# A spectral layer with maxout on one core: where a transform's columns land in PSUM, and when the next batch's first stage runs

## The chip, the cores and the metric

One Trainium2 chip, one of its cores. The time is device microseconds of one execution of the whole kernel; a kernel is judged by the median of its runs. Engines are named as in the profile: PE is TensorE (PEld its weight loads), DVE is VectorE, ACT is ScalarE, POOL is GpSimd, SP is SyncE, which here only issues DMAs.

## What is computed

A Fourier layer over 3072 time steps of 8 batches, 256 features wide, and a maxout layer behind it:

```python
X = np.fft.rfft(x, axis=1)                      # x: 8 x 3072 x 256
Yr = Xr @ w_r - Xi @ w_i + b_r                  # 256 x 256 weights
Yi = Xr @ w_i + Xi @ w_r + b_i
Yr, Yi = (np.sign(Y) * np.maximum(np.abs(Y) - 0.01, 0) for Y in (Yr, Yi))
y = np.fft.irfft(Yr + 1j * Yi, n=3072, axis=1)
h = np.maximum(np.maximum(y @ w1, y @ w2), y @ w3)   # 256 -> 768, three times
out = h @ w_out                                 # 768 -> 256
```

## The kernel before

Each batch's 3072 steps are split as 96 x 32 (n1 and n2), and every f32 matrix product is made of three f16 products (high part times high part, high times low, low times high: `mm3`, lines 176 to 178). A batch passes through these steps:

- **Stage a**, eight times a batch (one *quad* is four values of n2): `load_x` brings the rows of x by four DMAs of SP, `sum_x` adds or subtracts two halves on DVE (`xq`, line 529), `split_x` makes the high part on ACT and the low part on DVE (`xhl`), `stage_a` transforms over n1 by 12 matmuls into two PSUM tiles `pa` (line 572), copied out by two ACT instructions (`aq`, line 579) and written to DRAM by four DMAs of POOL.
- **Stage b**, twelve blocks a batch: `load_a` reads the rows back, `split_a` splits and moves them (`ab`), `stage_b` transforms over n2 by 16 matmuls into a PSUM tile `px` (line 731), each 128 rows by 64 columns. The last of the twelve blocks is *plain*: it is laid out in another way, as is all of batch 0.
- **Stage w** multiplies by the weights (tiles `py`), adds the bias and applies the threshold (`u`); `finish_w` splits the result (`vb`), and its rows are moved by four DMAs of SP (line 850) to where **stage q** needs them. Stage q takes two blocks at once, by 12 matmuls into two PSUM tiles `pz` (line 886), which ACT copies out (`zs`), to DRAM.
- **The inverse over n1** (`load_z`, `split_z`, `inverse`: tiles `zh`, `zl`, then `pi`, evacuated as `yh` by ACT and `yl` by DVE) and **the maxout layer** (`up`: tiles `pu`; `down`: tiles `pd`) for eight chunks of six *slots* each.

The last step sets the order of everything else: the main loop runs over 8 batches x 48 slots. In a slot stand three groups of 6 matmuls of `up` (which ACT `c`, line 980, then DVE `c`, line 983, and DVE `h`, line 986, read out of PSUM) and 9 matmuls of `down`. The steps of the following batches are put between these groups: each is an event with a position in slots (`at(p, fn, ...)`), the list of events is sorted, and `run_until` issues what is due. For a batch whose stages b to q run from slot 48(b-1), stage b of block k+1 stands at 2.8(k+2) + 1 behind that slot, stage q of a pair at 2.8(k+2) + 3.2 for even k: both every 5.6 slots. The quads of batches 3 to 7 come every 5.6 slots too, one batch of slots ahead of that batch's stage b. An instruction put off with `later` is issued some thirds of a slot later; the final order on each engine is that of the scheduler, and each engine runs its instructions in that order.

PSUM: `up` has three tiles, `down` two, and all others (`pa`, `px`, `py`, `pz`, `pi` and `pt`, by `ff_tile`) share three in turn, so a tile can be written once the third tile before it has been read out. SBUF: `xq` has two buffers; the second half of x, `ab` and `vb` share eight (`raw_tile`).

Of the kernel before, what the change touches and what calls it, by code (L numbers as in the profile page):

```python
# [98 lines left out]
def fourier_maxout_kernel(  # L99
    ctx: ExitStack, tc: tile.TileContext, x, w_r, w_i, b_r, b_i, w1, w2, w3, w_out, fa, ga, mb, mq, ident, out  # L100
):
    nc = tc.nc
# [4 lines left out]
    KD = D // P  # L107
# [5 lines left out]
    SLOTS = NCH * NF  # L113
# [28 lines left out]
    def later(fn):  # L142
        if "slot" in st:
            waiting.append((st["slot"], fn))
        else:
            fn()
# [17 lines left out]
    def split_later(hi, lo, src, scale=None):  # L164
        h = hi if hi.dtype == F16 else hi.bitcast(F32)
        if scale is None:
            nc.scalar.activation(out=hi, in_=src, func=AF.Copy)
            later(lambda: nc.vector.tensor_tensor(out=lo, in0=src, in1=h, op=ALU.subtract))
        else:
            nc.scalar.activation(out=hi, in_=src, func=AF.Copy, scale=scale)  # L170
            later(lambda: low(nc.vector.scalar_tensor_tensor(  # L171
                out=lo, in0=src, scalar=scale, in1=h, op0=ALU.mult, op1=ALU.subtract
            )))
# [9 lines left out]
    def ff_tile(name):  # L183
        tag = spare[0]
        if len(spare) > 1:
            spare.append(spare.pop(0))
        return ps.tile([P, 512], F32, name=name, tag=tag, bufs=2 if tag == "dn" else 3)
# [24 lines left out]
    def raw_tile(name):  # L212
        return ffn.tile([P, 1536], F32, name=name, tag="raw", bufs=8)
# [4 lines left out]
    def s_tile(name):  # L218
        return fft.tile([P, D], F32, name=name, tag="s", bufs=3)
# [230 lines left out]
    def at(pos, fn, i, k=None, n=None):  # L450
        if n is None or 0 <= k < n:
            events.append((pos, len(events), fn, i))

    def batch(b, kind):
        if (b, kind) not in st:
            if kind in "az":
                st[b, kind] = dram.tile([96, N2, D], F32, name=kind + "_d")
            else:
                w = 2 * NCH if kind == "x" else NJP if b else 2 * NJP
                st[b, kind] = fft.tile([P, w], F32, name="mx" + kind, bufs=3)  # L460
        return st[b, kind]
# [186 lines left out]
    def plain(k):  # L648
        return k < NJP or k % NJP == NJP - 1


    def first_b(k):
        aj = st.pop(("a", k))
        px = ff_tile("px")
        pv = px.rearrange("p (h j m) -> p h j m", h=KD, j=2)
        for j in range(2):
            for h in range(KD):
                nc.tensor.matmul(
                    pv[:, h, j], aj[:, j, h * P:(h + 1) * P], mb_f[:, 2 * k + j], start=True, stop=True
                )  # L660
        st["t", k] = t = fft.tile([P, KD, 384], F32, name="tf", tag="t2", bufs=2)
        tv = t.rearrange("p h (j m) -> p (h j) m", j=2)
        nc.scalar.activation(
            out=tv[:, :, 64:192], in_=px.rearrange("p (g m) -> p g m", m=P), func=AF.Copy
        )
        nc.scalar.activation(
            out=tv[:, :, 0:64], in_=px.rearrange("p (g m) -> p g m", m=P)[:, :, 64:128], func=AF.Copy,
            scale=-1.0,
        )
        if k == NJP - 1:  # L670
            st["ts"] = s_tile("tsf").rearrange("p (h m) -> p h m", h=KD)
            st["late"] = nc.gpsimd.tensor_copy(out=st["ts"], in_=t[:, :, 192:320])
            for z in (32, 96):
                nc.gpsimd.memset(st["ts"][:, :, z:z + 1], 0.0)
# [43 lines left out]
    def stage_b(k):  # L718
        if k < NJP:
            return first_b(k)  # L720
        ah = st.pop(("as", k))
        kb = k % NJP
        px = ff_tile("px")
        if plain(k):
            pv = px.rearrange("p (h j c q m) -> p h c j q m", h=KD, j=2, c=2, q=2)
        else:
            pv = px.rearrange("p (h c q m j) -> p h c j q m", h=KD, c=2, j=2, q=2)
        for g in range(4):
            for h in range(KD):
                for i in range(2):  # L730
                    nc.tensor.matmul(  # L731
                        pv[:, h, :, g // 2, g % 2], ah[:, g // 2, g % 2, h * P:(h + 1) * P],
                        mb_sb[:, i, 4 * kb + g].rearrange("p (c m) -> p c m", c=2),
                        start=i == 0, stop=i == 1,
                    )
        t2 = fft.tile([P, 2, KD, 384], F16, name="tt", tag="t2", bufs=2)
        st["t", k] = tt = [t2[:, i] for i in range(2)]
        if not plain(k):
            split_later(
                *(t[:, :, 0:256] for t in tt), px.rearrange("p (h m) -> p h m", h=KD), T_SCALE  # L740
            )
            pc = px.rearrange("p (h c m) -> p h c m", h=KD, c=2)
            s = s_tile("s").rearrange("p (h m) -> p h m", h=KD)
            nc.scalar.activation(out=s, in_=pc[:, :, 0, :], func=AF.Copy, scale=T_SCALE)

            def third():
                nc.vector.scalar_tensor_tensor(
                    out=s, in0=pc[:, :, 1, :], scalar=T_SCALE, in1=s, op0=ALU.mult, op1=ALU.add
                )
                split_later(*(t[:, :, 256:384] for t in tt), s)  # L750

            later(third)
            return
        tv = [t.rearrange("p h (j m) -> p (h j) m", j=2) for t in tt]
        split_later(*(t[:, :, 64:192] for t in tv), px.rearrange("p (g m) -> p g m", m=P), T_SCALE)

        def rest():
            for t in tv:
                nc.gpsimd.tensor_scalar(
                    out=t[:, :, 0:64], in0=t[:, :, 128:192], scalar1=-1.0, scalar2=1.0,  # L760
                    op0=ALU.mult, op1=ALU.mult,
                )
            sp = []
            for t in tt:
                s = fft.tile([P, D], F16, name="ts", bufs=2).rearrange("p (h m) -> p h m", h=KD)
                nc.gpsimd.tensor_copy(out=s, in_=t[:, :, 192:320])
                for z in (32, 96):
                    nc.gpsimd.memset(s[:, :, z:z + 1], 0.0)
                sp.append(s)
            st["ts"] = sp  # L770

        later(rest)
# [63 lines left out]
    def finish_w(k):  # L836
        b, kb = divmod(k, NJP)
        u = st.pop(("u", k))
        st["v", k] = u
        if b:  # L840
            if plain(k) or kb % 2 == 0:
                st["vb"] = raw_tile("vb").bitcast(F16)
            v = st["vb"][:, 2048:3072].rearrange("p (i j d) -> p i j d", i=2, j=2)
            moved = st["vb"][:, 0:2048].rearrange("p (g i j d) -> p g i j d", g=2, i=2, j=2)
            split_later(v[:, 0], v[:, 1], u, st[b, "sv"][0])

            def move():
                for j in range(2):
                    for c in range(2):
                        nc.sync.dma_start(out=moved[c::2, kb % 2, :, j], in_=v[j::2, :, c])  # L850

            if not plain(k):
                later(move)
            st["v", k] = [v[:, i] for i in range(2)] if plain(k) else moved
            nc.vector.tensor_reduce(
                out=batch(b, "u")[:, kb:kb + 1], in_=u.rearrange("p j d -> p (j d)"), axis=AX.X,
                op=ALU.max, apply_absolute_value=True,
            )
# [41 lines left out]

    for q in range(EARLY, NB * NCH):
        b, i = divmod(q, NCH)
        p = i if b == 1 else 9 + 5.2 * i if b == 2 else (b - 2) * SLOTS + 5.6 * i + 2
        at(p - (3 if b == 1 else 5 if b == 2 else 8), load_x, q)
        if q >= HALF_X:
            at(p - 1, sum_x, q)
        at(p, split_x, q)
        at(p + 1, stage_a, q)
        if q >= HALF_X:
            p = 9 + 5 * i if b == 3 else (b - 3) * SLOTS + 5.5 * i + 5  # L910
            at(p - 4, load_m, q)
            at(p, largest_m, q)
            if i == NCH - 1:
                at(p + 1, scale_m, b)
    for b in range(1, NB):
        for k in range(-2, NJP + 1):
            p = 8 + 2.2 * (k + 2) if b == 1 else (b - 1) * SLOTS + 2.8 * (k + 2)
# [291 lines left out]
```

## Time and profile before

| | us |
|---|---|
| median of 3 runs | 2040.73 (2039.59, 2040.73, 2047.87) |
| the profiled execution's own time | 2044.31 |
| its span in the profile | 2042.3 |

The profile is of one execution. Its first 139 us load, split and transform batch 0; then come eight stretches of about 247 us, one for each batch of the maxout layer, the last two of them shorter since no batches are left to prepare. Where one engine is busy nearly all the time, the time goes down only where that engine does less or waits less.

### The profile page before, as it was taken

To read this page: it belongs to the slowest core of one execution; us is meant where nothing else is said; L and a number is where in the kernel's file an instruction comes from. 1 tells how busy PE (TensorE), PEld (TensorE's weight loads), DVE (VectorE), ACT (ScalarE), POOL (GpSimd) and SP (SyncE) were. 2 spreads that over 40 slices of the span, in tenths; PEclk is the share of its full clock that TensorE was granted. 3 is DMA by queue.
4 is the path that set the end of the run, shared out by engine and by line. 5 is a ranking of instruction groups with operands and counts; after the bars stand their busy time and mean duration, and the time that the engine had idled before them with its cause. 6 is when DMAs were issued, how large, how long until landed. Compare 5 with 4: busy or idle time off the path is not lost.

```text
span 2042.3 us, 42196 instructions
## 1 busy us (share of the span) xinstructions
PE 2015.8 (99%) x16335; PEld 1406.8 (69%) x16335; DVE 1487.7 (73%) x2809; ACT 1036.1 (51%) x2060; POOL 282.5 (14%) x510
## 2 busy tenths in 40 slices
PE   9989999999999999999999999999999999999999
PEld 5757777676766766666766767667667677776666
DVE  3887887788877878678876788767777577754544
ACT  4755554555545554455554565545554454543333
POOL 0000101111111121111121121211121100100000
PEclk9999999999999999999999999999999999999999
DMA  8745444465443554545544454443542333211110
GB/s 278 212 147 155 142 128 118 126 158 132 130 143 95 144 159 107 145 119 139 142 133 113 124 162 120 140 117 89 152 123 70 88 92 88 81 58 32 32 32 24
DMA packets 183798, 244.66 MB, mean 120 GB/s; under 512 B 26350, under 2 KB 142702, under 8 KB 183502
## 3 DMA queue, kind: packets, MB, share of 16 engines
q1 hardware_dynamic: 150798, 166.44, 31.2%
q0 software_dynamic: 25168, 68.59, 10.1%
q10 hardware_dynamic: 7632, 6.95, 1.1%
q8 instruction: 128, 2.10, 0.4%
q14 instruction: 72, 0.59, 0.1%
HBM read 124.16 MB, written 75.50 MB: 98 GB/s over the span
## 4 chain that ended last, share of the span: by engine, by line
PE 87%; DVE 3%; DMA 3%; issue 3%; ACT 2%; SPq 1%; POOL 0%; ACTq 0%; DVEq 0%; POOLq 0%
PE pu L176 17%; PE pu L178 17%; PE pu L177 17%; PE pd L178 6%; PE pd L177 6%; PE pd L176 6%; PE px L731 3%; PE py L178 2%; PE py L176 2%; PE py L177 2%; PE pz L886 1%; PE pa L589 1%; PE pi L178 1%; PE pi L176 1%; PE pi L177 1%
## 5 line engine op out<-in xcount | busy, mean ns | idle before, releaser
L176 PE MATMUL pu<-yh,wuh 128*128 128x384 f16 x2304 | 754.7, 328 | 1.4 <-ACT c L980 0.7
L178 PE MATMUL pu<-yh,wul 128*128 128x384 f16 x2304 | 751.5, 326 | 0.0
L177 PE MATMUL pu<-yl,wuh 128*128 128x384 f16 x2304 | 751.4, 326 | 0.0
L170 ACT ACTIVATE hh<-h 128x384 f16<-128x384 f32 x384 | 200.7, 523 | 579.1 <-DVE h L986 566.6
L983 DVE TENSOR_TENSOR c<-pu,c 128x384 f32<-128x384 f32 x384 | 212.6, 554 | 187.6 <-PE pu L178 156.3
L178 PEld LDWEIGHTS <-wul 128*128 128x128 f16 x2304 | 225.4, 98 | 149.8 <-issue 0.9
L176 PEld LDWEIGHTS <-wuh 128*128 128x128 f16 x2304 | 227.6, 99 | 141.8 <-issue 30.4
L176 PE MATMUL pd<-woh,hh 128*128 128x256 f16 x1152 | 313.8, 273 | 0.0
L177 PE MATMUL pd<-wol,hh 128*128 128x256 f16 x1152 | 313.8, 273 | 0.0
L178 PE MATMUL pd<-woh,hh 128*128 128x256 f16 x1152 | 313.4, 273 | 0.0
L171 DVE SCALAR_TENSOR_TENSOR hh<-h,hh 128x384 f16<-128x384 f32 x384 | 213.8, 557 | 131.8 <-ACT hh L170 129.2
L177 PEld LDWEIGHTS <-wuh 128*128 128x128 f16 x2304 | 227.8, 99 | 115.1 <-issue 3.6
L980 ACT ACTIVATE c<-pu 128x384 f32<-128x384 f32 x384 | 187.7, 489 | 140.1 <-PE pu L178 134.0
L986 DVE TENSOR_TENSOR h<-pu,c 128x384 f32<-128x384 f32 x384 | 211.8, 552 | 54.5 <-PE pu L178 51.6
L1017 POOL DMA_DIRECT2D out_dram<-o x189 | 104.6, 558 | 1054.3 <-ACT o L1015 1048.7
L176 PE MATMUL py<-wch,tt 128*128 128x256 f16 x504 | 137.4, 273 | 0.0
L178 PE MATMUL py<-wch,tt 128*128 128x256 f16 x504 | 137.4, 273 | 0.0
L177 PE MATMUL py<-wcl,tt 128*128 128x256 f16 x504 | 137.3, 272 | 0.0
L582 POOL DMA_DIRECT2D a_d<-aq x160 | 93.7, 590 | 309.7 <-ACT aq L579 307.0
L176 PEld LDWEIGHTS <-hh 128*128 128x128 f16 x1152 | 112.7, 98 | 33.8 <-issue 0.3
L177 PEld LDWEIGHTS <-hh 128*128 128x128 f16 x1152 | 112.7, 98 | 33.4
L178 PEld LDWEIGHTS <-hh 128*128 128x128 f16 x1152 | 112.7, 98 | 13.7 <-DVE hh L171 0.5
(226 smaller groups left out, 2854.1 us busy)
## 6 DMA issues: line engine op xcount, KB each, us to landing
zq<-z_d SPq DMA_DIRECT2D x63, 384.0 KB, 4.0
out_dram<-o POOLq DMA_DIRECT2D x189, 128.0 KB, 2.1
ab<-a_d SPq DMA_DIRECT2D x84, 256.0 KB, 4.3
ab<-ab SPq DMA_DIRECT2D x336, 64.0 KB, 2.2
vb<-vb SPq DMA_DIRECT2D x308, 64.0 KB, 2.5
z_d<-zs POOLq DMA_DIRECT2D x70, 256.0 KB, 3.9
xm<-in_x_dram SPq DMA_DIRECT2D x40, 384.0 KB, 3.7
a_d<-aq POOLq DMA_DIRECT2D x160, 96.0 KB, 2.9
```

The source lines that it names most:

```text
L170: nc.scalar.activation(out=hi, in_=src, func=AF.Copy, scale=scale)
L171: later(lambda: low(nc.vector.scalar_tensor_tensor(out=lo, in0=src, scalar=scale, in1=h, op0=ALU.mult, op1=ALU.subtract)))
L176: nc.tensor.matmul(o, lh, rh, start=start, stop=False, **kw)
L177: nc.tensor.matmul(o, lh, rl, start=False, stop=False, **kw)
L178: st["mm"] = nc.tensor.matmul(o, ll, rh, start=False, stop=stop, **kw)
L582: nc.gpsimd.dma_start(out=av[1 - r, :, :, n:n + 512], in_=o[64 * h:64 * h + 48])
L589: nc.tensor.matmul(pa[0:96], fr, xp, start=True, stop=True)
L731: nc.tensor.matmul(pv[:, h, :, g // 2, g % 2], ah[:, g // 2, g % 2, h * P:(h + 1) * P], mb_sb[:, i, 4 * kb + g].rearrange("p (c m) -> p c ...
L980: st["act"] = nc.scalar.activation(out=c1, in_=p, func=AF.Copy)
L983: st["dve"] = nc.vector.tensor_tensor(out=c1, in0=p, in1=c1, op=ALU.max)
L986: st["dve"] = nc.vector.tensor_tensor(out=h32, in0=p, in1=st["c1"], op=ALU.max)
L1017: q.dma_start(out=out_v[b, c, t], in_=o)
```

## The change

Three lines. The first changes the order of the columns of `px` in the eleven blocks of a batch that are not plain: before, the two values of j (index `g // 2`) are the innermost index, so that one matmul's 64 columns go to every second f32 of the PSUM tile; now j stands outside q and m, and the 32 columns of each half go side by side. The rows of `py`, `u` and `v` follow that order. The second line is the matching source of the moves of `v`: 64 adjacent partitions instead of every second one, 128 x 2 x 256 values in four DMAs as before, into every second partition as before. The third takes 2 off the position p of the quads of batches 3 to 7: `load_x` at p - 8, `sum_x` at p - 1, `split_x` at p and `stage_a` at p + 1 all come two slots sooner; `load_m` and `largest_m`, which have a p of their own, stay.

```diff
@@ stage_b
         if plain(k):
             pv = px.rearrange("p (h j c q m) -> p h c j q m", h=KD, j=2, c=2, q=2)
         else:
-            pv = px.rearrange("p (h c q m j) -> p h c j q m", h=KD, c=2, j=2, q=2)
+            pv = px.rearrange("p (h c j q m) -> p h c j q m", h=KD, c=2, j=2, q=2)
@@ finish_w
             def move():
                 for j in range(2):
                     for c in range(2):
-                        nc.sync.dma_start(out=moved[c::2, kb % 2, :, j], in_=v[j::2, :, c])
+                        nc.sync.dma_start(out=moved[c::2, kb % 2, :, j], in_=v[64 * j:64 * j + 64, :, c])
@@ the events of the quads
     for q in range(EARLY, NB * NCH):
         b, i = divmod(q, NCH)
-        p = i if b == 1 else 9 + 5.2 * i if b == 2 else (b - 2) * SLOTS + 5.6 * i + 2
+        p = i if b == 1 else 9 + 5.2 * i if b == 2 else (b - 2) * SLOTS + 5.6 * i
         at(p - (3 if b == 1 else 5 if b == 2 else 8), load_x, q)
```

What that does to the order, at three places of the fifth batch of slots (the same places come in the batches of slots 1 to 5, counted from 0).

**PE, slot 20 of the batch.** Before, a quad's stage a (`pa`, line 572, with the two tiles 16509 and 16510) stands right before a pair's stage q (`pz`, line 886, tiles 16530 and 16531):

```order
L572 LDWEIGHTS zeros_72
L572 MATMUL pa_16510<-xhl_16427,zeros_72 64x512
L886 LDWEIGHTS zeros_72
L886 MATMUL pz_16530<-vb_16181,zeros_72 64x512
L886 LDWEIGHTS zeros_72
L886 MATMUL pz_16530<-vb_16181,zeros_72 64x512
L886 LDWEIGHTS zeros_72
L886 MATMUL pz_16530<-vb_16181,zeros_72 64x512
L886 LDWEIGHTS zeros_72
L886 MATMUL pz_16531<-vb_16181,zeros_72 64x512
```

Now the same pair (tiles 16536 and 16537) follows the maxout layer's `pd`:

```order
L178 LDWEIGHTS hh_16341
L178 MATMUL pd_16520<-woh_83,hh_16341 128x256
L886 LDWEIGHTS zeros_72
L886 MATMUL pz_16536<-vb_16187,zeros_72 64x512
L886 LDWEIGHTS zeros_72
L886 MATMUL pz_16536<-vb_16187,zeros_72 64x512
L886 LDWEIGHTS zeros_72
L886 MATMUL pz_16537<-vb_16187,zeros_72 64x512
```

The quad's stage a has gone two slots ahead. The tiles that share the three PSUM buffers follow each other there before as py_16458, pa_16509, pa_16510, pz_16530, pz_16531, so pz_16531 takes the buffer of pa_16509; now as px_16373, py_16453, py_16479, pz_16536, pz_16537.

**PE, slot 35 of the batch.** Before, block 11 of stage b (`px`) follows a group of `up`:

```order
L178 LDWEIGHTS wul_82
L178 MATMUL pu_17688<-yh_17107,wul_82 128x384
L731 LDWEIGHTS ab_17206
L731 MATMUL px_17698<-mb_all_77,ab_17206 128x2x32
L731 LDWEIGHTS ab_17206
L731 MATMUL px_17698<-mb_all_77,ab_17206 128x2x32
```

Now a quad's stage a stands between the two:

```order
L572 LDWEIGHTS zeros_72
L572 MATMUL pa_17704<-xhl_17643,zeros_72 64x512
L731 LDWEIGHTS ab_17211
L731 MATMUL px_17724<-mb_all_77,ab_17211 128x2x32
L731 LDWEIGHTS ab_17211
L731 MATMUL px_17724<-mb_all_77,ab_17211 128x2x32
```

The tiles in the three shared buffers are there before pi_17593, py_17613, pi_17661, px_17698, and now pi_17668, pa_17703, pa_17704, px_17724: this `px` now takes the buffer of the second `pi` of slot 34, which ACT and DVE read out as `yh` and `yl`.

**DVE, slot 34 of the batch.** Before, from the slot's `c` to the read-out (`yl`) of that second `pi`:

```order
L983 TENSOR_TENSOR c1_17583<-pu_17632,c1_17583 128x384
L776 TENSOR_SCALAR t_17629<-u_17626 128x512
L986 TENSOR_TENSOR h32_17648<-pu_17641,c1_17583 128x384
L777 TENSOR_TENSOR u_17626<-u_17626,t_17629 128x512
L171 SCALAR_TENSOR_TENSOR hh_17650<-h32_17648,hh_17650 128x384
L855 TENSOR_REDUCE mxu_15743<-u_17626 128x1
L171 SCALAR_TENSOR_TENSOR vb_17537<-u_17626,s0v_11363,vb_17537 128x512
L171 SCALAR_TENSOR_TENSOR yl_17592<-pi_17661,yh_17591 128x384
```

And now:

```order
L983 TENSOR_TENSOR c1_17591<-pu_17634,c1_17591 128x384
L833 TENSOR_TENSOR u_17628<-u_17628,bias_ri_86 128x512
L171 SCALAR_TENSOR_TENSOR xhl_17643<-xq_16979,xx_14891,xhl_17643 112x512
L776 TENSOR_SCALAR t_17631<-u_17628 128x512
L171 SCALAR_TENSOR_TENSOR xhl_17643<-xq_16979,xx_14891,xhl_17643 112x512
L777 TENSOR_TENSOR u_17628<-u_17628,t_17631 128x512
L986 TENSOR_TENSOR h32_17655<-pu_17648,c1_17591 128x384
L171 SCALAR_TENSOR_TENSOR yl_17600<-pi_17668,yh_17599 128x384
```

The two `xhl` of the quad have moved in ahead of `yl`, while `hh`, `mxu` and `vb` have moved behind it; in slot 33, ahead of what is shown, the quad's two `xq` (line 529) have moved in as well.

## Rows read from the trace of the kernel before

**Rows 1.** The page's first part, busy time and share of the span of PE, its weight loads, DVE, ACT and POOL.

```profile
PE 2015.8 (99%) x16335; PEld 1406.8 (69%) x16335; DVE 1487.7 (73%) x2809; ACT 1036.1 (51%) x2060; POOL 282.5 (14%) x510
```

**Rows 2.** Busy time by stretch: the stretch, its length, then busy us (and instructions) of PE, PEld, DVE, ACT, POOL, the granted share of TensorE's full clock, the busy share of the DMA engines, GB/s. One batch of slots in the middle.

```profile
1126.00:1373.00 247.00, 244.99 (x2083) 171.57 (x2082) 192.31 (x356) 128.79 (x259) 41.90 (x74) 1.00 0.47 131
```

**Rows 3.** Waits of PE alone, longest in total first: the waiting tile and line, the releaser, us in total, times, longest.

```profile
PE pz L886 <- ACT aq L579: 10.1, 15, 1.1
PE pi L176 <- ACT zh L170: 2.4, 1, 2.4
...
PE px L731 <- DVE yl L171: 1.0, 1, 1.0
```

**Rows 4.** Timeline of PE at a block of stage b that is not plain, and the first matmul behind it: start us, us, instruction (x16: sixteen of them merged).

```profile
543.19 1.06 PE L731 MATMUL px<-mb_all,ab 128*128 128x64 f16 x16
544.06 0.35 PE L176 MATMUL pu<-yh,wuh 128*128 128x384 f16 x1
```

**Rows 5.** The same at a plain block, and the start of another batch's plain block, three batches later.

```profile
556.84 0.63 PE L731 MATMUL px<-mb_all,ab 128*128 128x64 f16 x16
557.31 0.33 PE L176 MATMUL pu<-yh,wuh 128*128 128x384 f16 x1
...
1297.94 0.63 PE L731 MATMUL px<-mb_all,ab 128*128 128x64 f16 x16
```

**Rows 6.** Line 731 alone, weight loads and matmuls of all 84 blocks: count, shortest, median and longest duration in ns, first and last start.

```profile
L731 PEld LDWEIGHTS <-ab x1344: 95/125/125, 172.3 to 1783.2; 128*128 128x128 f16 x192
L731 PE MATMUL px<-mb_all,ab x1344: 192/247/247, 172.5 to 1783.2; 128*128 128x64 f16 x192
```

**Rows 7.** Timeline of PE at a stage a and at a stage q that each stand alone.

```profile
1060.42 0.33 PE L177 MATMUL pu<-yl,wuh 128*128 128x384 f16 x1
1060.58 0.33 PE L178 MATMUL pu<-yh,wul 128*128 128x384 f16 x1
1060.84 0.84 PE L572 MATMUL pa<-xhl,zeros 48*64 48x512 f16 x12
1061.61 0.34 PE L176 MATMUL pu<-yh,wuh 128*128 128x384 f16 x1
...
1063.67 0.84 PE L886 MATMUL pz<-vb,zeros 64*64 64x512 f16 x12
1064.45 0.34 PE L176 MATMUL pu<-yh,wuh 128*128 128x384 f16 x1
```

**Rows 8.** Timeline of PE at the four places of one batch of slots where a stage q stands one group of `up` behind a stage a (the first and the last) or directly behind it (the two between); in brackets the idle time before and its releaser.

```profile
938.71 1.15 PE L886 MATMUL pz<-vb,zeros 64*64 64x512 f16 x12
939.79 0.34 PE L176 MATMUL pu<-yh,wuh 128*128 128x384 f16 x1
...
968.13 0.84 PE L572 MATMUL pa<-xhl,zeros 48*64 48x512 f16 x12
968.80 0.59 PE L886 MATMUL pz<-vb,zeros 64*64 64x512 f16 x3
970.01 0.84 PE L886 MATMUL pz<-vb,zeros 64*64 64x512 f16 x9 [0.61 <-ACT aq L579]
970.78 0.34 PE L176 MATMUL pu<-yh,wuh 128*128 128x384 f16 x1
...
999.11 0.84 PE L572 MATMUL pa<-xhl,zeros 48*64 48x512 f16 x12
...
1002.21 0.34 PE L176 MATMUL pu<-yh,wuh 128*128 128x384 f16 x1
...
1032.40 0.40 PE L886 MATMUL pz<-vb,zeros 64*64 64x512 f16 x2
...
1033.90 0.34 PE L176 MATMUL pu<-yh,wuh 128*128 128x384 f16 x1
```

**Rows 9.** Timeline of ACT at the second of these places.

```profile
968.75 0.72 ACT L170 ACTIVATE vb<-u,s0v 128x512 f16<-128x512 f32 x1
969.38 1.06 ACT L579 ACTIVATE aq<-pa 128x512 f32<-128x512 f32 x2
```

**Rows 10.** Timeline of DVE in slots 33 to 36 of the fifth batch of slots (the first row is slot 33's `h`, the fifth the `yl` of slot 34's second `pi`), and of PE at the group of `up` that writes again the buffer of slot 33's `h`.

```profile
1290.59 0.54 DVE L986 TENSOR_TENSOR h<-pu,c 128x384 f32<-128x384 f32 x1
...
1296.34 0.56 DVE L171 SCALAR_TENSOR_TENSOR hh<-h,hh 128x384 f16<-128x384 f32 x1
1296.81 0.68 DVE L855 TENSOR_REDUCE mxu<-u 128x1 f32<-128x512 f32 x1
1297.41 0.74 DVE L171 SCALAR_TENSOR_TENSOR vb<-u,s0v,vb 128x512 f16<-128x512 f32 x1
1298.07 0.55 DVE L171 SCALAR_TENSOR_TENSOR yl<-pi,yh 128x384 f16<-128x384 f32 x1
...
1299.00 1.54 DVE L529 SCALAR_TENSOR_TENSOR xq<-x,sign,xq 112x512 f32<-112x512 f32 x2
...
1303.19 1.42 DVE L171 SCALAR_TENSOR_TENSOR xhl<-xq,xx,xhl 112x512 f16<-112x512 f32 x2
...
1293.52 0.33 PE L176 MATMUL pu<-yh,wuh 128*128 128x384 f16 x1
```

**Rows 11.** The moves of `v` (line 850) by all their DMAs, from issue to landing, and the last of them ahead of the stage q at 968.80.

```profile
DMA to landing us min/median/max: 1.9/2.5/5.3
...
956.46 3.38 SPq L850 DMA_DIRECT2D vb<-vb  x4
```

## The prediction

> **What bounds the kernel now.** I read the page's busy shares first. PE is busy for 2015.8 of 2042.3 us, DVE for 73% and ACT for 51% [rows 1]. A share over the whole span hides stages, so I read the busy times by stretch next: in a batch of slots in the middle of the run PE is busy for 244.99 of 247.00 us, at the full granted clock (1.00, so 2.4 GHz) [rows 2]. So nearly all the time is PE's own, and there are two ways to shorten it: fewer nanoseconds for the same matmuls, or fewer waits between them. The list of PE's waits shows how little waiting the profile counts: the largest entry is stage q's `pz`, which waits for the read-out `aq` of stage a, 15 times and 10.1 us in all; everything else is 2.4 us or less [rows 3]. These 15 are three in each of five batches, the five in which the quads of batches 3 to 7 run. Last I read the timeline of PE at the places that the change touches, by starts alone: the ends of matmuls are modelled, so what a block costs is the time from its first start to the first start behind it.
>
> **Part one, the columns of `px`.** The trace has both layouts. A block that is not plain starts at 543.19 and the next matmul at 544.06: 0.87 us for 16 matmuls, 54 ns each [rows 4]. The plain blocks, which already write their columns side by side, take from 556.84 to 557.31: 0.47 us, 29 ns each [rows 5]. Both have the same 16 loads of 128x128 weights and the same 16 matmuls of 64 columns. The difference is 0.40 us a block. The change gives the plain blocks' spacing of columns to the 11 other blocks of batches 1 to 7, 77 in all: 77 x 0.40 = 30.8 us off PE. All of it counts, since the blocks lie in stretches in which PE has no idle time to give [rows 2]. Bounds: nothing, if something other than the columns makes the 54 ns; 30.8 if it is they. I take 30.8, since the plain blocks are the same instructions in the same kernel.
>
> What could make the 54 ns instead is the weight load. Its records have a median of 125 ns and a shortest of 95 [rows 6], yet loads and matmuls overlap, and the plain block gets sixteen of both into 0.47 us [rows 5]; a load stretched to 125 ns is then a load that waits for the matmul before it.
>
> The Trainium skill ("TensorE: Matmul & The Clock Gate", section on LDWEIGHTS) has a rule that speaks against this part: a load takes its number of columns divided by 1.2 GHz, by an estimate from it 107 ns for these 128, whatever the matmul writes, so 16 of them would take 1.7 us and the first term would be zero. Both kinds of block in this trace are shorter than that, so the trace doesn't agree.
>
> The readers of `px` on ACT and DVE read whole runs of 128 or 256 columns before and after, and cost the same. The rows of `u` and `v` come in another order, and only the source of the moves changes, from every second partition to 64 adjacent ones. No row shows exactly this pair; the moves before land 2.5 us after issue, at worst 5.3 [rows 11]. What would a slower move cost? The last of the moves ahead of the stage q at 968.80 has been issued by 959.84 (956.46 + 3.38) and lands at about 962.3, 6.5 us early. Even the worst landing, doubled, ends 1.6 us after that point, and at the median doubled nothing waits. I take zero.
>
> **Part two, the quads two slots sooner.** Each quad's events move together: four loads on SP, two sums on DVE, two splits each on ACT and DVE, 12 matmuls, two read-outs on ACT and four writes on POOL. PE's own work stays: a stage a that stands alone takes 0.77 us (1060.84 to 1061.61), a stage q alone 0.78, and PE spends 0.10 us more at the entry of such a block (0.26 from the last start before it, where 0.16 is usual) [rows 7].
>
> What goes is the meeting of the two. Both take two of the three shared PSUM tiles, so when stage q comes right behind stage a its second tile is the buffer of stage a's first, which ACT must read out; at the second place ACT is still at `vb` when stage a ends and reads out its two tiles from 969.38 to 970.44 [rows 9], and stage q goes on at 970.01, after the first [rows 8]. The profile counts 0.61 us as idle there; the starts say more. At the four places of a batch [rows 8]:
> - 938.71 to 939.79: 1.08 us instead of 0.78, 0.30 lost;
> - 968.13 to 970.78: 2.65 for both blocks. Apart they would take 0.77 + 0.78 and one more entry of 0.10, 1.65: 1.00 lost;
> - 999.11 to 1002.21: 3.10 instead of 1.65: 1.45 lost;
> - 1032.40 to 1033.90: 1.50 instead of 0.78: 0.72 lost.
>
> That is 3.47 us a batch and 17.4 us in five, against the 10.1 us that the list of waits has for them [rows 3]: the modelled ends hide the rest. In the new order no pair's stage q has a stage a among the three tiles ahead of it, so I take all 17.4. Bounds: 0 (another wait at the same places) and 17.4.
>
> **What comes in its place.** Stage a now stands right ahead of a block of stage b six times a batch. `px` takes one tile, not two, so it needs the third tile back from it, that is the tile before stage a's two. At five of the six places that was read out long ago. At slot 35 it is the second `pi` of slot 34, and there DVE is late: from the `h` at 1290.59 to the end of `yl` at 1298.62 it goes nearly from one instruction into the next [rows 10]. In the new order the quad's two `xq` (1.54 us) and two `xhl` (1.42) come ahead of that `yl`, and `hh`, `mxu` and `vb` (0.56, 0.68, 0.74) go behind it: 2.96 - 1.98 = 0.98 us later, 1299.60. `px` would start at 1297.94 [rows 5] plus stage a with its entry, 0.87 [rows 7], which is 1298.81, and so waits for about 0.8 us. In five batches 4.0 us. That such a wait exists is seen once: `px` waits 1.0 us for `yl` [rows 3]. Bounds: 0, if DVE catches up by then, and 1.5 us a batch, if the read-out on ACT is late too: 0 to 7.5.
>
> The other moves lie under cover. The loads of x move two slots ahead with their readers, so their lead stays; a slot is (1297.94 - 556.84) / 3 / 48 = 5.15 us [rows 5]. The first quad of batch 3 is now loaded before the last of batch 2 and takes the `xq` buffer in its place; that last load waits for a split of the same slot and still has five slots, 25 us. SP's and POOL's instructions are no more than before. On ACT two `aq` now come ahead of the read-out of `px`, 1.06 us [rows 9]; stage w reads that block 3.8 slots behind its stage b (2.8 + 2 - 1), some 19 us, and ACT has 118 us to spare in a stretch [rows 2], so nobody waits for it.
>
> **Sum.** -30.8 - 17.4 + 4.0 = -44.2 us. The profiled execution took 2044.31 us in its own time, so it would take 2000.1. It lies 3.6 us above the median of the runs, 2040.73, on which I put the forecast: 2040.73 - 44.2 = 1996.5, say 1997 us.
>
> **The rivals.**
> - *The waits of part two only change their place.* DVE is busy for 192 of 247 us [rows 2], and in slots 33 and 34 the quad adds its 2.96 us where DVE had no pause; were PE to lose some 3.5 us a batch there and in like places, part two would give nothing: 2040.73 - 30.8 = 2010. For it: the one place worked out above. Against: the read-outs of `up` have room (the `h` that ends at 1291.13 is needed at 1293.52, 2.4 us later [rows 10]), which is more than one move of 1.54 us takes.
> - *The 54 ns are not the columns.* If weight loads pace the blocks, or anything else that both layouts share, part one gives nothing: 2040.73 - 17.4 + 4.0 = 2027. Against: the 0.87 us beside the 0.47 [rows 4, 5]. This is where the rule of the Trainium skill above would lead.
> - *Slower.* The place is DVE's `c` and `h`, whose late end holds back the next group of `up`. All 40 moved quads would have to cost more than 48.2 / 40 = 1.2 us each to lose both gains. With a room of 2.4 us that takes a lag of 3.6 us at each quad, and a quad has 2.96 us of work on DVE: it decides only if all of that and another instruction come ahead of the same `h`. A time of 2051 or more would need 1.5 us a quad.
> - *Nothing changes.* Something that I don't see paces the slots, and the time stays near 2040. Against: PE's idle time in a stretch is 2 us of 247 [rows 2].
>
> **How the numbers follow.** My forecast, both gains less a small new wait: 0.78 (its own range 1990 to 2003: the new wait at its bounds gives 1992.5 and 2000, and the runs spread by 1 us below the median and 7 above). Waits moved: 0.14. Columns not the cause: 0.03. Nothing: 0.03. Slower: 0.02. The range of 1988 to 2011 takes in the first two cases and leaves out 0.08 and their tails. About 0.5%, 10 us, is what a measurement here can tell from no change: faster by more than that means under 2030.5, which the first three cases give, 0.95; same 0.03; slower 0.02.
>
> **What would show it.** Part one: every block of line 731 takes 0.47 us from its first start to the next matmul, and PE's matmuls there have one duration, near 192 ns. Part two: `pz` no longer stands in the list of PE's waits, and each stage q takes 0.78 us. The new wait: `px` waits for `yl`, five times, some 0.8 us each. I am wrong if the blocks stay at 0.87 us, if entries of `pu` waiting for DVE's `c` or `h` come up in PE's list, or if more places than the one at slot 35 hold `px` back.

## The result, and the profile after

The changed kernel takes 1993.38 us, the median of four runs (1992.19 to 1994.02), beside 2040.16 for the kernel before on the same chip: a ratio of 0.9762, with a 95% interval of 0.9738 to 0.9786. That is 46.8 us less; the forecast's sum was 44.2 less, which it put at 1997 us. The profiled execution took 1993.83 us in its own time, with a span of 1992.1.

The page's first part, which answers to [rows 1]:

```profile
PE 1973.4 (99%) x16335; PEld 1368.6 (69%) x16335; DVE 1482.1 (74%) x2809; ACT 1026.7 (52%) x2060; POOL 279.1 (14%) x510
```

The counts of instructions are those of before. PE's busy time is 42.4 us less and the share stays 99%: the kernel is as bound by PE as it was. One batch of slots, by stretch with the columns of [rows 2]:

```profile
1088.46:1327.54 239.08, 239.00 (x2082) 166.05 (x2080) 191.41 (x355) 127.22 (x259) 41.06 (x74) 1.00 0.51 135
```

A batch takes 239.08 us where it took 247.03 on the mean of three (741.10 / 3 from [rows 5]), 7.95 less. The granted clock is 1.00 in both, the 2.4 GHz level, so the clock has no part in it.

**The blocks of `px`.** Line 731 with all its loads and matmuls (count, shortest, median and longest ns), which answers to [rows 6], and PE's timeline at a block right behind a stage a:

```profile
L731 PEld LDWEIGHTS <-ab x1344: 95/98/100, 170.6 to 1732.8; 128*128 128x128 f16 x192
L731 PE MATMUL px<-mb_all,ab x1344: 189/193/203, 170.7 to 1732.8; 128*128 128x64 f16 x192
```

```profile
962.84 0.84 PE L572 MATMUL pa<-xhl,zeros 48*64 48x512 f16 x12
963.61 0.64 PE L731 MATMUL px<-mb_all,ab 128*128 128x64 f16 x16
964.09 0.33 PE L176 MATMUL pu<-yh,wuh 128*128 128x384 f16 x1
964.25 0.33 PE L177 MATMUL pu<-yl,wuh 128*128 128x384 f16 x1
```

The median matmul is recorded with 193 ns instead of 247, and a block takes 0.47 to 0.48 us (963.61 to 964.09) instead of the 0.87 of [rows 4]. The weight loads went from 125 ns to 98 with no change of their own, so the longer figure held time spent waiting behind the matmuls.

One part of a block's cost does not lie in the block. Before, the row behind those of [rows 4] was

```profile
544.25 0.33 PE L177 MATMUL pu<-yl,wuh 128*128 128x384 f16 x1
```

so the first matmul of `up` behind a slow block took 0.19 us from its start to the next (544.06 to 544.25), where it takes 0.16 now (964.09 to 964.25). By the starts of all records it is 190 ns behind each of the 77 slow blocks, and 163 behind the plain ones and behind every block now. Inside a slow block the matmuls follow each other by 55.8 ns, only the second comes 29 ns after the first; inside a fast one by 29.2. So each of the sixteen cost 26.7 ns more, the last of them at the expense of the matmul behind: 0.427 us a block, not 0.40.

**The meetings of stage a and stage q.** PE's waits, the first four, which answer to [rows 3], and two of the four places of [rows 8]:

```profile
PE pi L176 <- ACT zh L170: 2.4, 1, 2.4
PE pz L712 <- DVE col L262: 1.8, 1, 1.8
PE px L658 <- DMA aj<-a_d: 1.5, 2, 1.2
PE px L731 <- DVE yl L171: 1.4, 1, 1.4
```

```profile
973.96 0.84 PE L886 MATMUL pz<-vb,zeros 64*64 64x512 f16 x12
974.74 0.34 PE L176 MATMUL pu<-yh,wuh 128*128 128x384 f16 x1
...
1004.33 0.84 PE L886 MATMUL pz<-vb,zeros 64*64 64x512 f16 x12
1005.10 0.34 PE L176 MATMUL pu<-yh,wuh 128*128 128x384 f16 x1
```

The entry of `pz` behind `aq`, 10.1 us, is gone, and each stage q that takes two blocks lasts 0.77 or 0.78 us. The four entries that are left lie at the start of the run or at single places.

**What came in its place.** The list shows no new wait in the five batches, but the starts do. PE at slots 29 and 35 of the fifth batch of slots, and DVE ahead of each:

```profile
1231.07 1.09 PE L572 MATMUL pa<-xhl,zeros 48*64 48x512 f16 x12
1232.09 0.64 PE L731 MATMUL px<-mb_all,ab 128*128 128x64 f16 x16
...
1260.45 0.84 PE L572 MATMUL pa<-xhl,zeros 48*64 48x512 f16 x12
1261.37 0.63 PE L731 MATMUL px<-mb_all,ab 128*128 128x64 f16 x16
```

```profile
1230.74 0.74 DVE L171 SCALAR_TENSOR_TENSOR xhl<-xq,xx,xhl 112x512 f16<-112x512 f32 x1
...
1254.32 0.54 DVE L986 TENSOR_TENSOR h<-pu,c 128x384 f32<-128x384 f32 x1
...
1260.78 0.54 DVE L171 SCALAR_TENSOR_TENSOR yl<-pi,yh 128x384 f16<-128x384 f32 x1
```

At slot 29 stage a takes 1.02 us instead of 0.77: it starts at 1231.07, and the second half of its own low part, `xhl`, is being written until 1231.48. At slot 35 `px` starts 0.92 us behind stage a instead of 0.77, 0.05 us after the end of `yl` (1261.32). Together 0.40 us; in three of the five batches just these two come, with 0.04 more in the third quad's stage a. The first batch has 0.68, the last none. In all 1.98 us: 0.65 at the `px` of slot 35, 1.33 in stages a.

### The profile page after: what moved, and what is told of

Same layout as the page of the kernel before. It is cut to its first block, busy times and chain, and to the rows that moved or that the text cites. A ratio compares the mean times of both kernels' runs of the same rounds, so it can differ in the third digit from the quotient of the medians.

```text
span 1992.1 us, 42215 instructions
## 1 busy us (share of the span) xinstructions
PE 1973.4 (99%) x16335; PEld 1368.6 (69%) x16335; DVE 1482.1 (74%) x2809; ACT 1026.7 (52%) x2060; POOL 279.1 (14%) x510
## 4 chain that ended last, share of the span: by engine, by line
PE 90%; DVE 5%; DMA 3%; ACT 1%; issue 1%; SPq 0%; DVEq 0%; ACTq 0%
PE pu L176 18%; PE pu L178 18%; PE pu L177 18%; PE pd L178 6%; PE pd L176 6%; PE pd L177 6%; PE py L176 3%; PE py L177 3%; PE py L178 3%; PE px L731 2%; PE pa L572 1%; PE pz L886 1%; PE pa L589 1%; PE pi L178 1%; PE pi L176 1%; PE pi L177 1%
```

## The experiments

All were held against runs of the kernel before on their own chip: 2041.89 us for the columns alone, the quads alone, the even pairs and the columns four apart; 2041.76 for the moves alone, the meetings, the changed kernel again and all splits sooner; 2042.16 for the odd pairs and the two quads sooner.

**Each part alone.** First the columns with the matching moves, without the quads:

```diff
-            pv = px.rearrange("p (h c q m j) -> p h c j q m", h=KD, c=2, j=2, q=2)
+            pv = px.rearrange("p (h c j q m) -> p h c j q m", h=KD, c=2, j=2, q=2)
...
-  nc.sync.dma_start(out=moved[c::2, kb % 2, :, j], in_=v[j::2, :, c])
+  nc.sync.dma_start(out=moved[c::2, kb % 2, :, j], in_=v[64 * j:64 * j + 64, :, c])
```

> The kernel before with the new columns of px and the new source of the moves; the quads stay where they were. Theory (each part gives its own gain): 77 blocks lose 0.40 us each, 30.8 us, so about 2009.5 us against 2040.2; line 731 takes 0.47 us a block, and pz waits for aq 15 times as before. Rival (the columns don't set the 0.87 us, the whole gain of 46.8 us came with the quads): near 2040. Second rival (the parts help each other, so that shorter blocks alone only lengthen the waits of pz): 2015 to 2025.

Measured 2011.27 us, 30.6 less (ratio 0.9851, 0.9836 to 0.9867). Summed over all 1344 matmuls from each start to the next on PE, line 731 went from 69.98 us to 39.17: 30.8 less, which is the term of the prediction. The matmuls of `up` behind the 77 blocks gave 2.1 us more (190 to 163 ns each). The waits of `pz` were still there and a little longer, 0.95 us by the starts:

```profile
PE pz L886 <- ACT aq L579: 10.8, 15, 1.4
```

Then the quads alone:

```diff
-        p = i if b == 1 else 9 + 5.2 * i if b == 2 else (b - 2) * SLOTS + 5.6 * i + 2
+        p = i if b == 1 else 9 + 5.2 * i if b == 2 else (b - 2) * SLOTS + 5.6 * i
```

> The kernel before with the quads of batches 3 to 7 two slots sooner and nothing else. Theory: the blocks of line 731 stay at 0.87 us; pz leaves the list of PE's waits; by the starts of the changed kernel pa and pz together lost 16.5 us, so about 2024 us against 2040.2, and not 2030, which the 10.1 us of the list would give. Rival (the waits only change their place while px is slow, as the blocks of px then end later against DVE and ACT): 2035 to 2040.

Measured 2024.69 us, 17.2 less (0.9914, 0.9898 to 0.9929); `pz` has left the list and line 731 keeps its 247 ns. The two gains alone make 47.8 us, and both together made 46.8 and, in a second set of runs below, 48.0: the parts neither help nor hinder each other. The rival by which the waits only change their place would have shown here at 2035 to 2040.

**What about the columns costs.** Three layouts of the `px` of the kernel before, each with its moves unchanged; where the columns are paired, the moving operand is viewed in pairs too, its values in the same order. First pairs of columns:

```diff
-            pv = px.rearrange("p (h c q m j) -> p h c j q m", h=KD, c=2, j=2, q=2)
+            pv = px.rearrange("p (h c q a j e) -> p h c j q a e", h=KD, c=2, j=2, q=2, e=2)
...
```

> The kernel before, with the columns of px written in pairs: two neighbouring columns, then a gap of two. The moves are unchanged, so v's rows are permuted and the output is another; the work is the same. First theory (what costs is to go to a new pair of columns, 8 bytes, for each single column): pairs are as fast as runs, blocks of 0.47 us and about 2009.5 us. Second theory (any gap costs): blocks stay at 0.87 us and the time near 2040. The Trainium skill speaks for the first in one place ("Advanced Engine Details and Errata", section PSUM Cachelines: every two consecutive elements should be contiguous for best throughput) and for the second in another ("PSUM — Partial Sum Buffer", table at the top: any non-contiguous access pattern slows matmuls).

Measured 2011.50 us (0.9849, 0.9831 to 0.9866), the same as with columns all side by side. Then single columns four apart:

```diff
-            pv = px.rearrange("p (h c q m j) -> p h c j q m", h=KD, c=2, j=2, q=2)
+            pv = px.rearrange("p (h c m q j) -> p h c j q m", h=KD, c=2, j=2, q=2)
```

> The kernel before, with the columns of px written four apart instead of two apart; moves unchanged, so v's rows are permuted and the output is another; the work is the same. If each single column costs the same whatever the gap: blocks of 0.87 us and the time near 2040. If the cost grows with the gap: blocks above 0.87 us, at twice the extra (1.27 us) some 31 us above 2040, 2071.

Measured 2041.25 us (0.9997, 0.9988 to 1.0007): no dearer than two apart. Last pairs that begin at an odd column:

```diff
-            pv = px.rearrange("p (h c q m j) -> p h c j q m", h=KD, c=2, j=2, q=2)
+            pv = px.rearrange("p (h c q a s) -> p h c q a s", h=KD, c=2, q=2, s=4)
...
+                    j, q = divmod(g, 2)
...
-                        pv[:, h, :, g // 2, g % 2], ah[:, g // 2, g % 2, h * P:(h + 1) * P],
+                        pv[:, h, :, j, q] if plain(k) else pv[:, h, :, q, :, 0:4:3] if j else pv[:, h, :, q, :, 1:3],
+                        ah[:, g // 2, g % 2, h * P:(h + 1) * P],
...
```

> The kernel before with the columns of px in pairs that begin at an odd column: the first eight matmuls of a block write columns 1 and 2 of every four, the last eight columns 0 and 3, which in order of writing are 0, then 3 and 4, 7 and 8 and so on. Moves unchanged, so v's rows are permuted and the output is another; the work is the same. If a neighbour is all that a column needs: blocks of 0.47 us as with even pairs, 30.8 us below the kernel before, some 2010 us. If the two must share an aligned 8 bytes, as the Trainium skill's word "cachelines" would have it ("Advanced Engine Details and Errata", section PSUM Cachelines): blocks of 0.87 us and no change, some 2041 us.

Measured 2042.48 us (0.9999, 0.9989 to 1.0008). The matmuls of the blocks in these three kernels, in the order even pairs, four apart, odd pairs (one or two lines of code were added in two of them, so the line number differs):

```profile
L732 PE MATMUL px<-mb_all,ab x1344: 189/193/203, 170.0 to 1749.5; 128*128 128x64 f16 x192
```

```profile
L731 PE MATMUL px<-mb_all,ab x1344: 192/247/247, 170.2 to 1780.3; 128*128 128x64 f16 x192
```

```profile
L733 PE MATMUL px<-mb_all,ab x1344: 192/247/248, 171.9 to 1783.4; 128*128 128x64 f16 x192
```

Even pairs are as fast as whole runs, and odd pairs as slow as single columns, although both have the same neighbours, gaps and counts. In the odd pairs both halves of a block are slow, 55.8 ns from start to start: the first eight matmuls, which write columns 1 and 2 of every four and differ from the even pairs in the offset alone, and the last eight. So neither the gap nor having a neighbour decides, but whether two columns written one after the other fill an aligned 8 bytes of PSUM. (Columns 1 and 2 lie in one aligned 16 bytes, and that does not help.) The Trainium skill ("Advanced Engine Details and Errata", section PSUM Cachelines) says that these lines hold two f32 and that every two consecutive elements should be contiguous; with the alignment that the word implies, these runs agree. The same section, and the table in "PSUM — Partial Sum Buffer" (section Specifications (TRN2)), also say that any non-contiguous pattern slows matmuls: the even pairs, 193 ns with gaps, do not agree.

**The moves of `v` alone.** Only the second hunk of the first diff:

> The kernel before with only the source of the moves changed, from every second partition to 64 adjacent ones; px keeps its columns, so v's rows are permuted and the output is another. Theory (the moves are hidden, and no slower): the same as before, 2040, landing 2.5 us after issue. Rival (64 adjacent partitions are read more slowly): a later landing, at twice the time 5 us, still with no effect on the total; above 3 us of effect the forecast's zero for the moves is wrong.

Measured 2040.55 us (0.9993, 0.9984 to 1.0002). All the moves of line 850, from issue to landing, there and then in the changed kernel:

```profile
DMA to landing us min/median/max: 2.0/2.6/5.7
```

```profile
DMA to landing us min/median/max: 2.0/3.0/5.2
```

They stand beside 1.9/2.5/5.3 of before [rows 11]: nothing that reaches the total, as the prediction had it.

**The meeting of stage a and stage q, made more frequent.** The changed kernel with

```diff
-        p = i if b == 1 else 9 + 5.2 * i if b == 2 else (b - 2) * SLOTS + 5.6 * i
+        p = i if b == 1 else 9 + 5.2 * i if b == 2 else (b - 2) * SLOTS + 5.6 * i + 2.2
```

and beside it the changed kernel unedited, on the same chip:

> The changed kernel with its quads placed so that stage a stands right ahead of stage q at all six places of a batch (before: twice right ahead and twice a third of a slot ahead). Theory (the meeting itself costs what the starts of the kernel before say, 1.00 to 1.45 us each): 5 to 6 meetings in five batches, 25 to 43 us above the changed kernel, less some 2 us for the small waits of px that go: 2016 to 2035. Rival (a meeting costs only what the list of waits has for it, 10.1 us / 15 = 0.67 us): 2008 to 2012. Second rival (the gain of the quads came from something else than that they no longer meet stage q): 1993 to 1998.

> The changed kernel itself, unedited, on the same chip as the two kernels that are held against it: 1993.4 us as before, within 1.5.

Measured 2024.57 us with the meetings and 1993.74 without: 30.8 us for 25 of them. By the trace five places of a batch meet and not six: the shorter stage q of the plain block has no stage a right ahead of it. PE's entry in the list and PE's timeline at one meeting:

```profile
PE pz L886 <- ACT aq L579: 21.1, 25, 1.4
```

```profile
1201.22 0.84 PE L572 MATMUL pa<-xhl,zeros 48*64 48x512 f16 x12
1201.89 0.59 PE L886 MATMUL pz<-vb,zeros 64*64 64x512 f16 x3
1203.10 0.84 PE L886 MATMUL pz<-vb,zeros 64*64 64x512 f16 x9 [0.61 <-ACT aq L579]
1203.86 0.34 PE L176 MATMUL pu<-yh,wuh 128*128 128x384 f16 x1
```

From 1201.22 to 1203.86 are 2.64 us for what takes 1.65 apart (as in the prediction): 0.99 lost where the list has 0.61. Over the 25 the same subtraction gives 1.0 to 1.8, 1.27 on the mean and 31.7 us in all. The 1.98 us of small waits are gone in this kernel, so by the starts it should be 29.7 slower, beside the 30.8 measured. The list's 21.1 are two thirds of the 31.7. So the meeting itself is the cause, and the starts are its price.

**Whether the two small waits can go.** The changed kernel with sums and splits of the quads one slot sooner and stage a where it was:

```diff
-            at(p - 1, sum_x, q)
-        at(p, split_x, q)
+            at(p - 2, sum_x, q)
+        at(p - (1 if q >= HALF_X else 0), split_x, q)
```

> The changed kernel with the two sums and the splits of the quads of batches 3 to 7 one slot sooner, their stage a where it is. Theory (stage a at slot 29 waits 0.25 us for its own split, and px at slot 35 waits 0.15 us for a split that those instructions hold up): both waits go, 5 x 0.40 = 2.0 us, so 1991.4. Rival (DVE's work one slot sooner holds up another split there): 1993 or a little more.

Measured 1999.07 us, 5.3 above the changed kernel: the theory falls as a forecast of the total. The waits at slots 29 and 35 are gone in its trace, but a dearer one has come at the batch's second quad. The list, and PE's and DVE's timelines there:

```profile
PE px L731 <- DMA ab<-ab: 3.9, 4, 1.2
```

```profile
1116.98 0.84 PE L572 MATMUL pa<-xhl,zeros 48*64 48x512 f16 x12
1118.79 0.92 PE L731 MATMUL px<-mb_all,ab 128*128 128x64 f16 x16 [0.97 <-DMA ab<-ab]
1119.55 0.33 PE L176 MATMUL pu<-yh,wuh 128*128 128x384 f16 x1
```

```profile
1110.38 1.41 DVE L171 SCALAR_TENSOR_TENSOR xhl<-xq,xx,xhl 112x512 f16<-112x512 f32 x2
...
1113.76 0.68 DVE L637 SCALAR_TENSOR_TENSOR ab<-ab 128x512 f16<-128x512 f32 x1
```

The quad's two `xhl` now come ahead of `ab`, which ends at 1114.44; its moves are issued behind it, and `px`, which could start at 1117.75, waits until 1118.79. In the changed kernel the same `ab` is done 7.7 us ahead of its `px`, here 4.35. By the starts `pa` and `px` together are 3.4 us dearer, 2.0 less for the old waits and 5.4 more for the new. The rest of the 5.3 us between the medians is not placed.

So sooner only for the two quads that gain by it:

```diff
+        early = q >= HALF_X and i in (5, 6)
-            at(p - 1, sum_x, q)
-        at(p, split_x, q)
+            at(p - 1 - early, sum_x, q)
+        at(p - early, split_x, q)
```

> The changed kernel with sums and splits one slot sooner for the two quads of a batch (the sixth and the seventh) whose stage a or next px waits, and not for the others. In the run with all quads sooner these two waits were gone and one new wait came, at the second quad, where px waits for its ab. Theory (the three have nothing to do with each other): 5 x (0.25 + 0.15) = 2.0 us below the changed kernel, 1991.5 by its 1993.5, with pa's time from start to start 2.0 us shorter. Rival (the sooner splits cost as much at these two places): 1993.5.

Measured 1992.00 us, ratio to the kernel before 0.9756 (0.9739 to 0.9773); the changed kernel had 0.9755 (0.9742 to 0.9769) in its second set. The totals can't be told apart. The trace shows the step: line 572 takes 1.53 us less from start to start (32.95 to 31.42), since the two waits are gone in four batches and one of 0.17 us came in the fifth. Whether this is the better kernel stays open; a gain of 1.5 us is below what the spread of these runs, 1989.80 to 1997.61, can show.

## Why the prediction was right, point by point

- **Columns, −30.8.** The mechanism was right, and the term a little too small. The starts of line 731 gave −30.8 and the medians −30.6 with that part alone, but 77 x 0.027 = 2.1 us more came at the matmul behind each block; against that, the waits of `pz` grew by 0.95 us in that run, and the changed kernel has none of them. "What a block costs is the time from its first start to the first start behind it" left this out: the slow writing of a block's last matmul delays the second start behind the block, not the first. The term is 77 x 0.427 = 32.9. The reason that it gave, the layout and not the weight load, holds: even pairs against odd pairs change nothing but the place of the columns. The rule on weight loads (the Trainium skill, "TensorE: Matmul & The Clock Gate", section on LDWEIGHTS: by an estimate from it 107 ns for 128 columns) does not pace these blocks, since they take a pair of load and matmul every 29 ns.
- **Moves, 0.** Right: 2040.55 beside 2041.76 with that edit alone.
- **Quads, −17.4.** Right, and so was the choice of the starts over the list's 10.1 us. Over all starts line 886 fell by 19.49 us, line 572 rose by 3.01, of which 1.98 are the new waits and the rest the ten stages a that had run straight into a stage q (0.67 us to the next start there, 0.77 alone), and the entries of those ten stages q cost `up` and `down` 10 x 0.09 = 0.93: −19.49 + 1.03 + 0.93 = −17.5. The quads alone gave −17.2 by the medians, with 0.85 us of new waits by the starts.
- **The new wait, +4.0.** The mechanism was right, the size was not. At slot 35 `px` does wait for `yl`, but by 0.15 us and not 0.8, and 0.65 us in all. These are the start of slot 34's second `pi` before and now, three rows of DVE before, and five now:

```profile
1295.48 0.21 PE L176 MATMUL pi<-ga_sb,zh 96*128 96x96 f16 x1
```

```profile
1257.89 0.21 PE L176 MATMUL pi<-ga_sb,zh 96*128 96x96 f16 x1
```

```profile
1291.05 0.68 DVE L637 SCALAR_TENSOR_TENSOR ab<-ab 128x512 f16<-128x512 f32 x1
1291.72 0.56 DVE L171 SCALAR_TENSOR_TENSOR hh<-h,hh 128x384 f16<-128x384 f32 x1
1292.48 0.56 DVE L171 SCALAR_TENSOR_TENSOR yl<-pi,yh 128x384 f16<-128x384 f32 x1 [0.20 <-ACT yh L170]
```

```profile
1253.00 1.40 DVE L529 SCALAR_TENSOR_TENSOR xq<-x,sign,xq 112x512 f32<-112x512 f32 x2
...
1258.05 0.74 DVE L171 SCALAR_TENSOR_TENSOR xhl<-xq,xx,xhl 112x512 f16<-112x512 f32 x1
1258.71 0.41 DVE L776 TENSOR_SCALAR t<-u 128x512 f32<-128x512 f32 x1
1259.05 0.73 DVE L171 SCALAR_TENSOR_TENSOR xhl<-xq,xx,xhl 112x512 f16<-112x512 f32 x1
1259.71 0.67 DVE L777 TENSOR_TENSOR u<-u,t 128x512 f32<-128x512 f32 x1
```

PE got to the place as computed, but DVE was not as late. Set against the start of that `pi`, `yl` ends 0.29 us later than before, where 0.98 was added up. That durations were added which overlap is not the reason: from start to start the two `xq` take 1.32 (1253.00 to `h` at 1254.32) and each `xhl` 0.66, while `hh`, `mxu` and `vb` took 1.73 [rows 10], which makes 0.91. The step that failed is "it goes nearly from one instruction into the next" [rows 10]. Between `h` and `yl` DVE still had pauses, 0.3 us of them at the `yl` of 1292.48, which waited for ACT's `yh`, and the rest in smaller pieces. Now these instructions follow each other without them, and 0.62 of the 0.91 us is gone.
- **One wait was missed.** "At five of the six places that was read out long ago" looked at `px` only. At slot 29 it is stage a itself that waits, 0.25 us, for its own low part: its split had moved with it, but into a place where DVE is late. Such waits of stage a make 1.33 of the 1.98 us, twice what the forecast wait at `px` came to.
- **Sum.** A batch of the kernel before takes 246.83 us from plain block to plain block; the 247.03 above is the mean of two such and one of 247.44, in which `pi` once waited 0.6 us for DVE's `zl`. Now it takes 239.08, 7.75 less, and the terms give 11 x 0.427 + 3.47 − 0.43 = 7.74. For the whole run they give −32.9 − 17.5 + 2.0 = −48.4, where the medians are 46.8 and 48.0 apart. The forecast lies 3.6 us above the measured median: 2.0 by the new waits, 2.1 by the columns and 0.5 by rounding 1996.5 up, together 4.6, less about 1 us, which is within what executions of one kernel differ by. Both errors were small and pointed the same way, so the forecast did not come out by one hiding the other.
- **The forecast's base.** Putting the sum on the median rather than on the profiled execution was right: the time before the first matmul of `up` differs between executions of one kernel. These are the matmuls of line 176 for `up` (shortest, median, longest ns, first and last start) in the kernel before and in the changed kernel's first and second profile:

```profile
L176 PE MATMUL pu<-yh,wuh x2304: 322/326/524, 112.2 to 2034.3; 128*128 128x384 f16 x192
```

```profile
L176 PE MATMUL pu<-yh,wuh x2304: 322/326/524, 110.9 to 1983.9; 128*128 128x384 f16 x192
```

```profile
L176 PE MATMUL pu<-yh,wuh x2304: 322/326/524, 115.2 to 1987.5; 128*128 128x384 f16 x192
```

From the first to the last start are 1922.1 us before, of which the one wait of `pi` for `zl` is 0.6, and 1873.0 and 1872.3 now; the 4.3 us between the first starts of the last two lie in the head.

## What to carry to other kernels

Price a block of matmuls from its first start to the next block's first start, and look whether the first matmul behind it takes longer than its like elsewhere, since what the block's last matmul costs can show there. A list of idle times takes the modelled ends for real and had two thirds of what the meetings here cost, and showed nothing of the small waits. Where an output of f32 columns must be interleaved, do it by pairs that begin at an even column, or leave the interleaving to a later DMA that is hidden. When work is moved sooner on an engine that is in order, look at what it is put ahead of, at each place that it moves to: the same edit took 0.4 us a batch away at two quads and cost 0.8 to 1.6 us a batch at a third.

## What the runs showed of the hardware

- A matmul of 64 f32 columns holds up the next one by 29.2 ns when each aligned 8 bytes of PSUM is filled at once, and by 55.8 when each is filled by halves (from start to start inside the blocks): 0.46 and 0.87 ns a column. The 26.7 ns between them are 0.417 a column, one period of the granted 2.4 GHz. The gap makes no difference: even pairs with a gap of two columns take 0.47 us a block as whole runs do, and single columns two or four apart both 0.87.
- A load of 128x128 f16 weights ahead of every matmul does not keep the blocks from 29 ns a pair: the loads are recorded with 98 ns each, so by the records several are under way at once. The Trainium skill ("TensorE: Matmul & The Clock Gate", section Back-to-back issue gap) has columns / 2.4 GHz + 2.5 ns for a single matmul, by an estimate from it 29 ns for 64, and says that this is too little for a stream of loads and matmuls; here the stream keeps to it.
